# Attention with routed experts: routing units spread over the steps by parity, and the experts' first transposes moved ahead of a value product

## The chip, the cores and the metric

The kernel runs on one core of one Trainium2 chip. The metric is the device time of one execution in microseconds (us), from the median of several runs.

## The reference, cut to what matters

```python
scores = scale * q @ k.T                     # B=4, H=8, S=768, D=64
scores = where(sink | window, scores, -1e9)  # 4 sink keys, the last 128 keys
a = exp(scores - max) / (sum + 1e-9)
x = (a @ v), heads side by side              # 3072 tokens x 512
g = argmax(x @ w_group); e = argmax(x @ w_expert[g])   # 4 groups x 4 experts
out[token] = p(g) * p(e) * (relu(x @ w1[g, e]) @ w2[g, e])
```

Every token goes to one expert of 16, with 512 inputs, 1024 hidden units and 512 outputs.

## The kernel before, in words

**Attention** is a loop of 26 steps (L1234). Steps 0 to 23 each start one tile of 128 queries of all 8 heads (six tiles to a batch element), and each works on three tiles at once: scores, row maxima and exponentials of tile i, transposes and value products of tile a = i-1, and the end of tile b = i-2. Every engine takes its instructions strictly in the order in which the loop writes them.

TensorE's order in a step is: `scores(i,0)`, `values(b,1)`, `scores(i,1)`, `sink_t(a)` and `trans(a,1)` (transposes of the probabilities), `natural(b)` (the output turned back into rows), `logits(b)`, `values(a,0)`, the routing batch's matmuls if there are any, `sink_values(a)`, `trans(i,0)`. In the trace these are `ps<-kb,qb`, `po<-pw,vv`, `tp<-ident,sp`, `tp<-ident,pt`, `po<-ident,xT`, `ps<-wsd,xT`, `tp<-oh,trib` and its followers, and `po<-spT,sv`.

VectorE's order is: `maxima(i,0)`, `maxima(i,1)` (`sm<-ps,msk`, after a copy `ps<-selu,ps`), in even steps `sums` (`rc`), `norm_logits(b)` (`lw<-ps,rc`), then `norm(b)` (`xt<-po,rc`), which divides the rows by their sums and lets the tile go to memory. `norm` reads the same banks of `po` that the next step's `values(b,1)` writes. ScalarE does the exponentials (`pt<-sm,st`), copies transposes out of PSUM (`evac`: `pw<-tp`; `sink_evac`: `spT`; `out_evac`: `xT<-po`) and the rounded halves of the experts' weights (`whi`); VectorE makes the rest of these weights (`wlo`) in steps from 18 on. GpSimd multiplies the probabilities by a triangular mask (`halves`: `pw<-pw,tri`, two a step) and adds up the heads' logits.

**Routing** is done in four batches of six tiles. `route_batch` (L364) is a generator whose pieces, the units, are small VectorE instructions. Their order is: maximum `m`, difference `d`, `req`, second maximum `m2`, comparison `eq`, one-hot `oh`; the matmuls ("pe"); `pe` and a copy of the counts ("rd"); for batches 1 and 2 the choice of an expert, `pick_id` (`ktmp`, `cs`, `key`, `ktop`, `ktmp`, `keid`, `eid`, `oh01`); `rs`, `runb`, `pos`, `ge`, `gs`, `ga`, `m0`, `rm`, `s5`, `rss`; two units HV1 and HV2 ("hv": `bf` on VectorE, `af` on GpSimd); matmuls ("pe") and the addition to the table `tab` ("rd"); `sel` and `index` (`gidx`, `idz`, `sidx`). Batches 0 to 2 become ready in steps 8, 14 and 20. Batches 0 and 1 keep intermediate tensors in free columns of the scores' PSUM tile `psb[1]` (`keep`, L376); batch 2 keeps most of them in SBUF.

A step has places at which units are taken:

```python
maxima(i, 1, lambda k: unit(k) if k else None)   # L1299: two units
routing(1, ("pe",))                              # L1316
for k in range(4): unit(k)                       # L1327: four, ahead of norm
norm(b)                                          # L1330
late()                                           # L1335: wlo of a weight chunk
routing(1, ("rd",)); routing(1, ("hv",))         # L1336, L1337
for k in range(2): unit(k)                       # L1338: two more
```

**The experts' entry.** In steps 24 and 25 the attention is finished while the first expert's work begins: `early_work` (L1215) transposes two gathered tiles of tokens (`ph<-ident,xg`, copied by ScalarE and VectorE into `un`) and then runs the first layer in pieces. After that the experts follow one another, TensorE reading weights as pairs `whi` and `wlo`.

Of the kernel before, what the change touches and what calls it, by code (L numbers as in the profile page):

```python
# [55 lines left out]
XLEAD = 9  # L56
PEGAP = 1.6
REND, TSTEP = 8, 16
UNITS = {}
HC = 3  # L60
LATE = 6
PELAG = 2.0
# [72 lines left out]
def moe_attention(tc, kqT, vN, vS, nsw, wgx, w1, w2, out):  # L135
    nc = Pinned(tc)
    v = nc.vector
    with ExitStack() as top, ExitStack() as att:
# [41 lines left out]
        def bank(pt):  # L180
            return pt.tile([P, 4, P], F32, name="tp")
# [7 lines left out]
        def spare():  # L189
            return tail[0].tile([P, 512], F32, name="ph")  # L190
# [162 lines left out]
        def put_gates(n):  # L353
            for _ in range(min(n, len(gates))):
                t, g = gates.pop(0)
                nc.sync.dma_start(xd[t * P:(t + 1) * P, DM:XW], g)
# [7 lines left out]
        def route_batch(i0, nb, lt, wk, pt, tab, na, pick=None):  # L364
# [35 lines left out]
            yield  # L400
            v.tensor_reduce(m, o5a, AX.X, ALU.max)
            yield
            og = psb[1][:, :, PART - nb:PART].rearrange("p c n -> p n c") if keep else o5[:, :, 0]
            if keep:
                o5b, mb = (t.rearrange("p a (b k) c -> p a b k c", k=nk) for t in (o5a, wide(m)))
                v.tensor_tensor(og.rearrange("p (a b) c -> p a b c", a=na2), o5b[:, :, :, 0], mb[:, :, :, 0], ALU.is_equal)
            v.tensor_tensor(o5a, o5a, wide(m), ALU.is_equal)
# [1 line left out]
            oh = wk.tile([P, nb, NE], BF16, name=f"oh{nb}", bufs=1)  # L409
            v.tensor_tensor(oh.rearrange("p n (g e) -> p n g e", g=G), o5[:, :, 1:],  # L410
                            og[:, :, :, None].to_broadcast([P, nb, G, EG]), ALU.mult)
            yield "pe"
            pp = misc(pt)
            pc = pp[:, nb * NE:(nb + 1) * NE]
# [458 lines left out]
        def values(i, g):  # L873
            pw = env[i]["pw", g]
            new, old = vts[i], vts.get(i - 1) if i % NT else None
            quarters(g, 0, P, new[:, 0], lambda d, j: pw[d, 2 * j:6 + 2 * j:5], start=g == 0)
            quarters(g, D, D, new[:, 1], lambda d, j: pw[d, 1 + 2 * j], stop=g == 1 and old is None)
            if old is not None:
                quarters(g, 0, P, old[:, 1], lambda d, j: pw[d, 4 + 2 * j:10 + 2 * j:5])
                quarters(g, 0, D, old[:, 0], lambda d, j: pw[d, 8 + 2 * j], stop=g == 1)  # L880

        def out_evac(i):
            env[i]["xT"] = xT = wk.tile([P, NDC, P], F32, name="xT", bufs=1)
            nc.scalar.copy(xT.rearrange("p (g l) q -> p l g q", l=2), po2[:, :, 0:256].rearrange("p l (g q) -> p l g q", g=2))
# [85 lines left out]
        def xpose(q, j, early=False):  # L970
            T, o = q["T"], q["o"]
            w = min(P, T - j * P)
            src = xg[q["r"], q["j0"] + j]
            cg[q["r"], q["j0"] + j] = gate = gp.tile([P, 1], F32, name="cg", bufs=10)
            tx = spare().rearrange("p (a b) -> p a b", a=NDC) if early else bank(ps_t)
            dve(0.3 + 0.5 * w / P)
            for c in range(NDC):
                nc.tensor.transpose(tx[:, c, 0:w], src[0:w, c * P:(c + 1) * P], ident[0:w, 0:w])
            if q["plain"]:
                q["x"] = a = yp.tile([P, NDC, 64], F32, name="xr", bufs=1)[:, :, 0:w]  # L980
                nc.scalar.copy(a, tx[:, :, 0:w])
                v.tensor_copy(gate[0:w], src[0:w, DM:DM + 1])
                return
            a = xx[:, :, o + j * P:o + j * P + w]
            nc.scalar.copy(a, tx[:, :, 0:w])
            v.tensor_tensor(xx[:, :, o + T + j * P:o + T + j * P + w], tx[:, :, 0:w], a.bitcast(F32), ALU.subtract)
            v.tensor_copy(gate[0:w], src[0:w, DM:DM + 1])
# [226 lines left out]

        def early_work(q):  # L1215
            plan.update(todo=[], at=0, next=0)
            for j in range(q["nt"]):
                xpose(q, j, True)
                yield 0.43
            for k, us in enumerate(layer1_wide(q)):  # L1220
                if k == LATE:
                    wait_for("late")
                    xpose(PARTS[0][1], 0, True)
                yield us
# [3 lines left out]
        def unit(k):  # L1228
            if quota[0] > 0 and routing(1, (None,)):
                quota[0] -= 1  # L1230

        ew = early_work(PARTS[0][0])
        load_s(0)
        for i in range(NI + 2):  # L1234
            live = i < NI
            quota[0] = UNITS.get(i, REND)
            a, b = i - 1, i - 2
            mid, old = 0 <= a < NI, 0 <= b < NI
            state["clk"] += 3.0
            if i == NI:  # L1240
                flush()
                state.update(gap=0.0, dve=state["clk"])
                sps.close()
                put_gates(MAXB)
                while later:
                    gather(*later.pop(0))
                ps_h = fl.enter_context(tc.tile_pool(name="ps_h", bufs=4, space=PSUM, side="right", reuse_waits="tile"))
                tail.append(ps_h)
            if live:
                scores(i, 0)  # L1250
            if mid:
                evac(a, 0)
            if i == NI and half:
                half.pop()()()
            if old:
                if b < NI - 1:
                    values(b, 1)
                out_evac(b)
            if live:
                load_v(i)  # L1260
                scores(i, 1)
                issue()
                maxima(i, 0)
                warm(FILL[i] if i < len(FILL) else 0, tp2[:, 0, 256:448])
            if mid:
                sink_copy(a)
                halves(a, 0)
            if i == NI + 1:
                state["at"] = 0.0
                routing(1, ("pe",))  # L1270
            if mid:
                if not live:
                    next(ew)
                    next(ew)
                sink_t(a)
                trans(a, 1)
            if live:
                exps(i, 0, (0, 1))
            if mid:
                evac(a, 1)  # L1280
                sink_evac(a)
            if live:
                exps(i, 0, (2, 3))
            if mid and not live:
                halves(a, 1)
            if not live and later and not gates:
                gather(*later.pop(0))
            late = None
            if live:
                late = half.pop()() if half else wjob()  # L1290
                if half and i % NT == 0:
                    first, more = late, half.pop()
                    late = lambda: (first(), more()())
            if i == 0:
                late_consts()
            if i == 1:
                routing_consts()
            if live:
                maxima(i, 1, lambda k: unit(k) if k else None)  # L1299
            if old:  # L1300
                natural(b)
            state["clk"] += 3.0
            if old:
                logits(b)
            if live and mid:
                values(a, 0)
            if i % 2 == 0 and 0 < i <= NI:
                sums(i - 1)
            if not live:
                norm(b)  # L1310
                norm_logits(b)
                next(ew)
            if mid and not live:
                values(a, 0)
            add_heads()
            routing(1, ("pe",))  # L1316
            if mid:
                sink_values(a)
            if live and old:
                norm_logits(b)  # L1320
            if live:
                if mid:
                    halves(a, 1)
                flush()
                exps(i, 1)
                trans(i, 0)
                for k in range(4):  # L1327
                    unit(k)
                if old:
                    norm(b)  # L1330
                if later and not gates:
                    gather(*later.pop(0))
                put_gates(2)
                if late:
                    late()  # L1335
                routing(1, ("rd",))  # L1336
                routing(1, ("hv",))  # L1337
                for k in range(2):  # L1338
                    unit(k)
            else:  # L1340
                if mid:
                    values(a, 1)
                    next(ew)
                put_gates(MAXB)
                routing(TSTEP, (None, "rd", "hv"))
            if old:
                del env[b]
            if i >= CHOOK:
                prefetch(min(RAW, len(raws) + (1 if live else RAW)))
            if not live:  # L1350
                wjob()
                next(ew, None)
# [295 lines left out]
```

## Time and profile before

| | us |
|---|---|
| median of 3 runs | 487.92 |
| lowest and highest run | 487.7, 488.58 |
| the profiled execution | 487.55 |
| its span, first to last instruction | 485.7 |
| TensorE busy | 462.8 (95%) |
| VectorE busy | 341.5 (70%) |
| ScalarE busy | 325.9 (67%) |
| GpSimd busy | 163.8 (34%) |

The span is what the trace covers; 1.85 us of the profiled execution lie around it. Attention takes the first 147 us or so, the experts the rest. An engine's idle time before an instruction is printed in brackets in the timeline, with what ended it.

### The profile page before, as it was taken

To read this page: it belongs to the slowest core of one execution; us is meant where nothing else is said; L and a number is where in the kernel's file an instruction comes from. 1 tells how busy PE (TensorE), PEld (TensorE's weight loads), DVE (VectorE), ACT (ScalarE), POOL (GpSimd) and SP (SyncE) were. 2 spreads that over 40 slices of the span, in tenths; PEclk is the share of its full clock that TensorE was granted. 3 is DMA by queue.
4 is the path that set the end of the run, shared out by engine and by line. 5 is a ranking of instruction groups with operands and counts; after the bars stand their busy time and mean duration, and the time that the engine had idled before them with its cause. 6 is when DMAs were issued, how large, how long until landed. Compare 5 with 4: busy or idle time off the path is not lost.

```text
span 485.7 us, 15514 instructions
## 1 busy us (share of the span) xinstructions
PE 462.8 (95%) x5865; PEld 394.7 (81%) x5865; DVE 341.5 (70%) x1143; ACT 325.9 (67%) x875; POOL 163.8 (34%) x269
## 2 busy tenths in 40 slices
PE   7999999998879999999999999999999999999994
PEld 6887778776768987989888778797979788877894
DVE  6766787888897799893075256563788888788870
ACT  4898889889884353772265275655778787687961
POOL 3463675565656022323203033012402160205021
PEclk9999999999999999999999999999999999999999
DMA  6566567577764469795124388858969997968200
GB/s 192 162 200 206 192 181 215 181 232 259 263 203 137 132 202 360 242 360 217 47 70 148 109 282 289 306 218 305 381 216 373 410 384 249 301 210 298 63 26 31
DMA packets 49556, 107.47 MB, mean 221 GB/s; under 512 B 8932, under 2 KB 9444, under 8 KB 49472
## 3 DMA queue, kind: packets, MB, share of 16 engines
q1 hardware_dynamic: 45008, 93.17, 56.7%
q0 software_dynamic: 4320, 12.94, 7.7%
q8 instruction: 48, 0.79, 0.7%
q10 hardware_dynamic: 144, 0.28, 0.2%
q14 instruction: 36, 0.29, 0.2%
HBM read 93.58 MB, written 12.93 MB: 219 GB/s over the span
## 4 chain that ended last, share of the span: by engine, by line
PE 65%; DVE 13%; issue 8%; ACT 6%; DMA 4%; POOL 2%; SPq 1%; POOLq 0%; DVEq 0%; ACTq 0%
PE po L105 29%; PE ph L105 28%; PE tp L105 4%; PE ps L105 4%; DVE wlo L105 3%; ACT pt L105 2%; DVE sm L105 2%; DVE xt L105 2%; ACT whi L105 1%; DMA rw<-in_w 1%; DVE un L105 1%; DMA vv<-in_vN 1%; DVE ps L105 1%; DMA ni<-in_nsw 1%; SPq L105 1%
## 5 line engine op out<-in xcount | busy, mean ns | idle before, releaser
L105 DVE TENSOR_TENSOR wlo<-rw,whi 128x1024 fp32r<-128x1024 f32 (+1 forms) x116 | 134.9, 1187 | 28.3 <-ACT whi L105 27.9
L105 PE MATMUL ph<-un,whi 128*128 128x256 f32 (+9 forms) x576 | 128.8, 313 | 0.1
L105 PE MATMUL po<-whi,un 128*128 128x512 f32 (+6 forms) x384 | 126.3, 394 | 0.0
L105 ACT CAST whi<-rw 128x1024 fp32r<-128x1024 f32 (+1 forms) x116 | 114.8, 1018 | 5.7 <-PE po L105 3.5
L105 POOL DMA_INDIRECT out<-ot,sidx x33 | 41.7, 1264 | 221.0 <-ACT ot L105 164.3
L105 PE MATMUL ph<-un,wlo 128*128 128x160 f32 (+10 forms) x416 | 99.6, 265 | 0.2 <-DVE wlo L105 0.2
L105 PEld LDWEIGHTS ph<-un,whi 128*128 128x128 f32 x576 | 94.0, 189 | 2.4 <-issue 0.6
L105 PEld LDWEIGHTS po<-whi,un 128*128 128x128 f32 (+5 forms) x384 | 69.8, 183 | 19.3 <-issue 2.1
L105 ACT ACTIVATE pt<-sm,st 128x136 f32<-128x136 f32 x192 | 76.2, 404 | 7.9 <-DVE st L105 7.7
L105 PE MATMUL po<-wlo,un 128*128 128x512 f32 (+7 forms) x200 | 77.9, 389 | 0.0
L105 PEld LDWEIGHTS ph<-un,wlo 128*128 128x128 f32 x416 | 76.8, 190 | 0.8 <-DVE wlo L105 0.4
L105 POOL TENSOR_TENSOR pw<-pw,tri 128x512 f32<-128x512 f32 x40 | 51.6, 1289 | 17.9 <-ACT pw L105 17.0
L105 DVE CUSTOM_DVE_ANT_0 sm<-ps,msk 128x136 f32<-128x136 f32 x192 | 46.3, 296 | 7.2 <-ACT xT L105 1.4
L105 PE MATMUL po<-pw,vv 64*64 64x128 f32 (+1 forms) x1408 | 40.9, 250 | 7.0 <-POOL sp L105 2.3
L105 PEld LDWEIGHTS po<-pw,vv 64*64 64x64 f32 x1408 | 34.9, 133 | 13.4 <-POOL sp L105 8.2
L105 POOL DMA_INDIRECT xg<-xd,gidx x33 | 35.1, 1065 | 29.4 <-DMA rw<-in_w 16.1
L105 PE MATMUL ps<-kb,qb 64*64 64x204 f32 (+1 forms) x768 | 41.9, 331 | 3.1 <-DVE bf L105 2.1
L105 PEld LDWEIGHTS po<-wlo,un 128*128 128x128 f32 (+6 forms) x200 | 35.7, 179 | 7.8
L105 DVE TENSOR_TENSOR hc<-ph,hc 128x160 f32<-128x160 f32 (+6 forms) x64 | 21.5, 337 | 26.2 <-ACT hc L105 26.2
L105 ACT ACTIVATE un<-ph 128x256 fp32r<-128x256 f32 (+1 forms) x40 | 15.3, 383 | 36.4 <-PE ph L105 36.0
L105 ACT ACTIVATION_READ_ACCUMULATOR pt<-sm,st 128x1 f32 x192 | 37.2, 194 | 0.0
L105 ACT ACTIVATE ot<-po,cg 128x512 f32<-128x512 f32 (+7 forms) x25 | 17.0, 679 | 29.3 <-PE po L105 29.2
(226 smaller groups left out, 654.6 us busy)
## 6 DMA issues: line engine op xcount, KB each, us to landing
rw<-in_w SPq DMA_DIRECT2D x128, 512.0 KB, 5.9
kb<-in_kqT SPq DMA_DIRECT2D x23, 272.0 KB, 4.6
qb<-in_kqT SPq DMA_DIRECT2D x24, 256.0 KB, 3.7
vv<-in_vN SPq DMA_DIRECT2D x24, 256.0 KB, 3.7
xd<-xt SPq DMA_DIRECT2D x24, 256.0 KB, 2.7
xg<-xd,gidx POOLq DMA_INDIRECT x33, 5.8
out<-ot,sidx POOLq DMA_INDIRECT x33, 5.9
sv<-in_vS SPq DMA_DIRECT2D x4, 128.0 KB, 3.7
```

The costliest lines, as they stand in the source:

```text
L105: r = f(*a, **k)
```

## The change

It takes out `UNITS` (an empty table, so the quota of 8 units a step stays). It gives the comparison that makes `oh` a PSUM operand in batch 2 as well (`early` in place of `keep`), at one more small instruction. In steps with i % 6 = 3 it takes one unit in the middle of `maxima(i,0)`. Ahead of `norm` it takes up to 4 units in odd steps, 2 in even ones and 1 where i % 6 = 2; an "hv" unit may now be taken there and counts four. After `norm` the "rd" unit comes first, then `late` and two units, or the units first where the next one is "hv". In step 24 the transposes of both token tiles, `sink_copy`, the first `halves` and `trans(a,1)` are written ahead of `values(b,1)`, and `evac(a,1)`, the second `halves` and the copies of the token tiles ahead of `out_evac(b)`; the second half of a weight chunk comes after `sink_evac`.

```diff
@@ route_batch
-            og = psb[1][:, :, PART - nb:PART].rearrange("p c n -> p n c") if keep else o5[:, :, 0]
-            if keep:
+            og = psb[1][:, :, PART - nb:PART].rearrange("p c n -> p n c") if early else o5[:, :, 0]
+            if early:
                 o5b, mb = (t.rearrange("p a (b k) c -> p a b k c", k=nk) for t in (o5a, wide(m)))
                 v.tensor_tensor(og.rearrange("p (a b) c -> p a b c", a=na2), o5b[:, :, :, 0], mb[:, :, :, 0], ALU.is_equal)
...
+            og = og if keep else o5[:, :, 0]
             yield "pe"
@@ early_work
-            for j in range(q["nt"]):
-                xpose(q, j, True)
-                yield 0.43
+            both = []
+            for j in range(q["nt"]):
+                both.append(spare().rearrange("p (a b) -> p a b", a=NDC))
+                for c in range(NDC):
+                    nc.tensor.transpose(both[j][:, c], xg[q["r"], j][:, c * P:(c + 1) * P], ident)
+            yield 0.86
+            for j in range(q["nt"]):
+                xpose(q, j, both[j])
+            yield 0.0
@@ a new function
+        def fill(n, kinds=(None, "hv")):
+            while n > 0 and quota[0] > 0:
+                big = bool(rb) and rb[0][2] == "hv"
+                if not routing(1, kinds):
+                    return
+                n -= 4 if big else 1
+                quota[0] -= 1
@@ the loop of steps
-            if i == NI and half:
-                half.pop()()()
+            if i == NI:
+                next(ew)
+                sink_copy(a)
+                halves(a, 0)
+                trans(a, 1)
             if old:
                 if b < NI - 1:
                     values(b, 1)
+                if i == NI:
+                    evac(a, 1)
+                    halves(a, 1)
+                    next(ew)
                 out_evac(b)
+            if i == NI:
+                sink_t(a)
+                sink_evac(a)
+                if half:
+                    half.pop()()()
...
-                maxima(i, 0)
+                maxima(i, 0, lambda k: unit(k) if k == 1 and i % NT == 3 else None)
...
-                for k in range(4):
-                    unit(k)
+                fill((2, 1, 4)[i % 2 * 2 if i % NT != 2 else 1])
                 if old:
                     norm(b)
...
+                routing(1, ("rd",))
+                if late and not (rb and rb[0][2] == "hv"):
+                    late()
+                    late = None
+                    kinds = None,
+                else:
+                    kinds = None, "hv"
+                fill(2, kinds)
                 if late:
                     late()
-                routing(1, ("rd",))
-                routing(1, ("hv",))
-                for k in range(2):
-                    unit(k)
```

The calls of step 24 that stand earlier now (`sink_copy`, `halves`, `sink_t`, `trans`, `evac`, `sink_evac`) are taken out of their old places, which the other steps keep.

## Rows read from the trace of the kernel before

**Rows 1.** Windows: length, busy PE, PEld, DVE, ACT, POOL; clock, DMA, GB/s.

```profile
49.40:55.90 6.50, 5.45 (x150) 4.52 (x146) 5.71 (x30) 4.89 (x22) 5.08 (x8) 1.00 0.51 182
...
150.00:250.00 100.00, 99.09 (x708) 88.59 (x707) 67.96 (x191) 45.94 (x81) 26.93 (x32) 1.00 0.59 200
```

**Rows 2.** Timeline of PE, steps 8 and 9: start, length, instruction, idle before.

```profile
54.94 0.90 PE L105 MATMUL po<-pw,vv 64*64 64x128 f32 x32 [1.05 <-DVE ps L105]
...
57.77 0.90 PE L105 MATMUL po<-pw,vv 64*64 64x128 f32 x32
58.60 0.22 PE L105 MATMUL tp<-oh,trib 128*128 128x96 bf16 x1
```

**Rows 3.** Timeline of DVE, steps 8 and 9.

```profile
52.97 0.28 DVE L105 TENSOR_REDUCE ps<-lt 128x30 f32<-128x120 f32 x1
...
54.11 0.68 DVE L105 TENSOR_TENSOR xt<-po,rc 128x512 f32<-128x512 f32 x1
...
55.23 0.26 DVE L105 TENSOR_TENSOR oh<-req,ps 128x96 bf16<-128x96 f32 x1
...
59.75 0.69 DVE L105 TENSOR_TENSOR xt<-po,rc 128x512 f32<-128x512 f32 x1 [1.13 <-ACT pt L105]
```

**Rows 4.** Timelines of PE and DVE, steps 10 and 16.

```profile
66.93 0.90 PE L105 MATMUL po<-pw,vv 64*64 64x128 f32 x32 [0.53 <-DVE row L105]
...
100.26 0.33 DVE L105 TENSOR_REDUCE ps<-oh 128x16 f32<-128x96 bf16 x1
...
101.57 0.90 PE L105 MATMUL po<-pw,vv 64*64 64x128 f32 x32 [0.80 <-DVE xt L105]
```

**Rows 5.** Waits of PE, 44 to 150 us (total, times, longest); one DVE row.

```profile
PE ps L105 <- DVE bf L105: 2.1, 2, 1.6
...
PE ps L105 <- DVE sidx L105: 0.8, 1, 0.8
...
111.19 0.69 DVE L105 TENSOR_TENSOR xt<-po,rc 128x512 f32<-128x512 f32 x1 [0.89 <-PE po L105]
```

**Rows 6.** Timelines of DVE, POOL and ACT, steps 21 to 24.

```profile
132.77 1.33 DVE L105 TENSOR_TENSOR oh<-req 128x96 bf16<-128x96 f32 x1
...
140.10 0.17 DVE L105 SCALAR_TENSOR_TENSOR key<-cnt,col 128x16 f32<-128x16 f32 x1
...
143.25 0.82 DVE L105 SCALAR_TENSOR_TENSOR ktmp<-key,ktop,col 128x16 f32<-128x16 f32 x1
...
144.97 0.17 DVE L105 TENSOR_TENSOR runb<-runb,rs 128x16 bf16<-128x16 bf16 x1
...
138.23 0.69 DVE L105 TENSOR_TENSOR xt<-po,rc 128x512 f32<-128x512 f32 x1 [0.49 <-DMA rw<-in_w]
...
146.60 1.01 DVE L105 TENSOR_TENSOR ge<-row,edge 128x48 f32<-128x48 f32 x1
...
132.58 1.41 POOL L105 TENSOR_TENSOR pw<-pw,tri 128x512 f32<-128x512 f32 x1 [0.28 <-ACT pw L105]
...
140.54 1.29 POOL L105 TENSOR_TENSOR pw<-pw,tri 128x512 f32<-128x512 f32 x1 [0.96 <-ACT pw L105]
...
139.88 0.58 ACT L105 COPY pw<-tp 128x512 f32<-128x512 f32 x1 [0.47 <-DVE cnt L105]
```

**Rows 7.** Timelines of PE and ACT, step 24.

```profile
145.92 0.90 PE L105 MATMUL po<-pw,vv 64*64 64x128 f32 x32 [1.67 <-POOL sp L105]
146.75 1.09 PE L105 MATMUL ph<-ident,xg 128*128 128x128 f32 x8
...
148.13 0.41 PE L105 MATMUL po<-ident,xT 64*128 64x64 f32 x8
...
145.49 0.57 ACT L105 COPY pw<-tp 128x512 f32<-128x512 f32 x1
...
146.87 0.59 ACT L105 COPY xT<-po 128x512 f32<-128x512 f32 x1 [0.30 <-PE po L105]
147.44 1.07 ACT L105 CAST un<-ph 128x512 fp32r<-128x512 f32 x2
```

More of the change, by code (lines that the diff above doesn't have):

```diff
@@ L58 @@
 REND, TSTEP = 8, 16
-UNITS = {}
 HC = 3
@@ L974, in xpose @@
             cg[q["r"], q["j0"] + j] = gate = gp.tile([P, 1], F32, name="cg", bufs=10)
-            tx = spare().rearrange("p (a b) -> p a b", a=NDC) if early else bank(ps_t)
+            tx = early if early not in (True, False) else spare().rearrange("p (a b) -> p a b", a=NDC) if early else bank(ps_t)
             dve(0.3 + 0.5 * w / P)
-            for c in range(NDC):
+            for c in range(NDC if early in (True, False) else 0):
                 nc.tensor.transpose(tx[:, c, 0:w], src[0:w, c * P:(c + 1) * P], ident[0:w, 0:w])
@@ L1235, in moe_attention @@
             live = i < NI
-            quota[0] = UNITS.get(i, REND)
+            quota[0] = REND
             a, b = i - 1, i - 2
@@ L1262, in moe_attention @@
                 issue()
-                maxima(i, 0)
+                maxima(i, 0, lambda k: unit(k) if k == 1 and i % NT == 3 else None)
                 warm(FILL[i] if i < len(FILL) else 0, tp2[:, 0, 256:448])
-            if mid:
+            if live and mid:
                 sink_copy(a)
@@ L1270, in moe_attention @@
                 routing(1, ("pe",))
[L1271 to L1274, printed above, removed]
+            if live and mid:
                 sink_t(a)
@@ L1278, in moe_attention @@
                 exps(i, 0, (0, 1))
-            if mid:
+            if live and mid:
                 evac(a, 1)
@@ L1283, in moe_attention @@
                 exps(i, 0, (2, 3))
-            if mid and not live:
-                halves(a, 1)
             if not live and later and not gates:
```

## The prediction

> **What bounds the kernel now.** I read the windows first, one step of attention and then the stretch behind it. In the step from 49.4 to 55.9 us no engine is full: TensorE is busy for 5.45 of 6.5 us [rows 1]. From 150 to 250 us TensorE is busy for 99.09 of 100 us [rows 1]. So whatever attention and the experts' entry gain or lose moves the end one for one. Next I read TensorE's timeline for its idle time. In step 9 (the even steps' sums have just been made) `values` starts after 1.05 us of idle time [rows 2]. The timeline of VectorE names the cause: `norm` (`xt<-po,rc`) starts at 54.11, behind four units, and ends at 54.79; `values`, which writes the banks that `norm` reads, follows 0.15 later [rows 2, 3]. Step 14 repeats this pattern; steps 10 and 16 lose 0.53 and 0.80 us in the same place [rows 4]. In the steps with weight work two other waits stand out: scores wait 2.1 us in all for `bf` and 0.8 for `sidx` [rows 5], since those read `psb[1]`. Last, I looked for VectorE instructions that are longer than their like. `oh` takes 1.33 us in batch 2 where it takes 0.26 in batch 0, `ktmp` 0.82 and `ge` 1.01; each lies beside a GpSimd multiply of some 1.3 us and ends with it [rows 3, 6]. Only batch 2, whose operands both lie in SBUF, shows this.
>
> **The parts, step by step** (later is +).
>
> *Steps 8 and 14: 0.* One unit instead of four stands ahead of `norm`. `m` ends at 53.25, so `norm` can start 0.94 us earlier than 54.11 and `values` too [rows 2, 3]. But `m2`, `eq` and `oh` now lie among the maxima of the next step, and the routing matmuls follow in that same step, ahead of `sink_values`. VectorE has the same six units and two maxima to do before those matmuls as before, in another order, with `oh` at the end; before, that work was done when `lw` started, which was ahead of an idle 1.13 us up to the `norm` at 59.75 [rows 3]. `m2` must also wait for scores that share its bank. By this count `oh` ends at about 58.45 and the matmul starts 0.15 later, at 58.6; it started at 58.60 before, right behind `values` at 57.77 [rows 2]. TensorE's wait has moved from `norm` to the one-hot. Bounds: -0.94 and +0.2 each.
>
> *Step 10: -0.25.* Two units leave the front of `norm`; of the 0.53 us [rows 4] some 0.45 can go. HV1 and HV2 now fall into one step, so GpSimd does two `af` ahead of the next `sink_copy` and `halves`, which gives back 0.2. Bounds -0.53 and 0.
>
> *Step 16: -0.47.* `rs` (0.33) and `runb` (0.17, priced by batch 2's) go behind `norm` [rows 4, 6], less a little overlap. Bounds -0.80 and 0.
>
> *Steps 18 to 20: -0.25.* HV1 moves into the 0.89 us that VectorE idles before `norm` in step 18 [rows 5] and HV2 ahead of the weights' `wlo`, so the 2.1 us of waiting for `bf` go. VectorE's queue, not the scores, then sets the next step, and the table matmuls, `tab`, `sel` and `index` come one step earlier: the 0.8 us for `sidx` [rows 5] come back there. Bounds: -2.1 and +0.6.
>
> *Steps 20 and 21: +0.64.* As in step 8 the one-hot gates the routing matmuls, now in step 21 rather than 22, so that what the last three parts won is nearly used up at the `norm` of step 21. Bounds 0 and +0.9.
>
> *Step 21 behind `norm`: +0.68.* Before, `wlo` and the held `oh` took 1.9 us until the next maxima, 1.33 of it `oh`. With the one-hot's operand in PSUM the 1.07 us of excess go. In its place come `pe`, `cnt`, `wlo`, `ktmp`, `cs` and two `key`. ScalarE's `evac` waits for `cnt`, takes 0.58, and the multiply starts 0.08 behind it (140.54 against 139.88 + 0.58, [rows 6]); with 0.1 from `cnt` to `evac` that is 0.76 after `cnt`. `wlo` and the two small ones, now behind `cnt`, take some 0.83, and then comes `key`, which reads two SBUF tensors: it waits for the multiply's 1.29 [rows 6]. From `norm` on this makes 0.35 for `pe` and `cnt`, 0.76, 1.29 and 0.2 for the second `key`: 2.6 against 1.9. The 0.83 and the 0.35 are my estimates from the small instructions' 0.17 to 0.25 and what is left of the 1.9. Bounds: -1.07 (no meeting) and +0.8.
>
> *Step 22: +0.5, then +0.5.* In this step with sums nothing stood ahead of `norm`; now `ktop`, `ktmp` (0.82 beside a multiply, [rows 6]), `keid`, `eid` and `oh01` do, some 1.2 us with overlap; 0.49 of that was idle [rows 6] and 0.2 more is taken off as the routing matmuls have left the step. Behind `norm`, `wlo`, `rs` and `runb` replace `wlo` and six short instructions. `evac` no longer waits for `cnt` (0.47, [rows 6]), so the multiply is under way when `runb` (0.17 when free) wants to read two SBUF tensors. Bounds of each: 0 and +1.3.
>
> *Step 23: -0.15.* `ge` beside a multiply replaces `ktmp` beside one, the rest is equal in size.
>
> *Step 24: +0.8.* TensorE idled 1.67 us before `values` [rows 7]; the tokens' transposes (1.09) and `trans` now lie in that time. But `xT`, on which `natural` waits, now stands behind more on ScalarE: from the end of the exponentials at 145.5, `evac` 0.57, `trans` 0.42 with two waits of 0.1 (it shares the banks that `evac` reads), `evac` 0.57, the casts 1.07, `xT` 0.59 and 0.1 to TensorE [rows 7]: 148.9, where `natural` was at 148.13. VectorE and ScalarE shift a little against each other, hence -0.05. Behind it TensorE's work is the same. The weight casts that go later are covered by this wait. Bounds: -1.0 (all of the transposes' 1.09 saved) and +1.2. The batch's earlier progress costs nothing and buys nothing: its matmuls in step 25 waited for nothing.
>
> The sum is -0.25 - 0.47 - 0.25 + 0.64 + 0.68 + 0.5 + 0.5 - 0.15 + 0.8 = **+2.0 us**, on the profiled execution's 487.55: 489.55. The median of the runs stands 0.37 above that execution, so I forecast 489.9.
>
> *A rule beside the rows.* Three instructions were held by 1.07, 0.6 and 0.8 us, a mean of 0.82; priced so, `key` and `runb` together would cost 0.7 us less than I put. The Trainium skill, SBUF — State Buffer, "Who interferes with whom", says that an instruction of VectorE with two SBUF inputs and a reading one of GpSimd lock each other out for the whole instruction, whichever began first. By that rule both wait out what is left of the multiply, as in the sum above; by the mean alone the time would be 489.2. The ends of `oh` and of its multiply (134.10 and 133.99, [rows 6]) agree with the rule.
>
> **The rivals.**
>
> *No meeting.* If VectorE gets to `key` and `runb` before the multiplies begin (`key` misses by 0.07 us in my count), the 0.68 and one 0.5 fall away: 489.9 - 1.2 = 488.7, within 0.2% of before. For it: `key` ran freely at 140.10 [rows 6]. Against: `runb` misses by 0.4.
>
> *Faster.* VectorE is ahead of my count by some 0.7 us in each batch, because TensorE's earlier scores let it start sooner. Its place is the one-hot in steps 9, 15 and 21. From 0.7 us on, the routing matmuls find it ready, and the 0.94, 0.94 and 0.64 us stay won; batch 2 then slips ahead of its multiplies too, another 1.2: 489.9 - 3.7 = 486.2. For it: VectorE idles 1.13 us in step 9 [rows 3], so it isn't full. Against: that idle time lies behind the one-hot, not ahead of it.
>
> *Step 24 as meant.* If `trans` needn't wait for `evac` and `xT` gets through, the entry gives -1.0 instead of +0.8: 488.1, no change.
>
> **How the numbers follow.** The three runs span 0.9 us, so about 0.2% (1 us) can be told from no change. The forecast has 0.48, the two rivals near zero 0.20 together, the faster one 0.32. The slower side reaches to 491.4 if both held instructions take the upper bounds; the faster one to 485.2, with the entry's gain on top. Outside that I leave 2 in 10. Alone, the likeliest case runs from 489.0 to 491.4.
>
> **What would show it.** Right: in steps 9 and 15 `values` without the 1.05 us of idle time, and an idle stretch of some 0.5 us before `tp<-oh,trib` instead; `oh` of batch 2 at 0.26; a `key`, `runb` or `ge` of over 0.8; in step 24 the tokens' transposes before `values` and TensorE waiting over 1 us for `xT`. Wrong: routing matmuls that start without waiting in step 9, steps 21 to 23 no longer than before, or `natural` in step 24 less than 3 us behind the exponentials.

## The result, and the profile after

The changed kernel takes **492.99 us** in the median of four runs (491.41 to 494.5), beside 487.81 for the kernel before in the same comparison: a ratio of **1.0105 [1.0069, 1.0141]**. It is slower, as forecast, but by 5.2 us and not by 2, and outside the range.

The profiled execution is the shortest of the four, 491.41 us. Its page begins with the span and the busy times, then the span in 40 slices of 12.24 us:

```profile
span 489.6 us, 15516 instructions
...
PE 466.1 (95%) x5865; PEld 397.0 (81%) x5865; DVE 341.5 (70%) x1144; ACT 325.6 (66%) x875; POOL 164.7 (34%) x269
...
PE   7999999997888999999999999999999999999994
...
PEclk9999999999988999999999999999999999999998
```

Against the table of before, VectorE, ScalarE and GpSimd are as busy as they were. TensorE has the same 5865 instructions but 3.3 us more busy time, and the line of its clock shows why: two slices, from 135 to 159 us, are not at full clock (the third is the very end). The page of before has a 9 in every slice.

To see where the 3.9 us of span came from, I took the starts of `xT<-po` from ScalarE's timeline, one for each step, and compared their distances:

| from `xT` of step to step | before, us | after, us | difference | forecast |
|---|---|---|---|---|
| start to 8 (nothing changed) | 49.44 | 48.66 | -0.78 | 0 |
| 8 to 10 | 12.15 | 12.12 | -0.03 | 0 |
| 10 to 12 | 11.60 | 11.26 | -0.34 | -0.25 |
| 12 to 14 | 10.53 | 10.73 | +0.20 | none |
| 14 to 16 | 12.41 | 12.84 | +0.43 | 0 |
| 16 to 18 | 11.78 | 11.43 | -0.35 | -0.47 |
| 18 to 22 | 25.41 | 25.84 | +0.43 | +0.39 |
| 22 to 23 | 7.05 | 8.59 | +1.54 | +1.68 |
| 23 to 24 | 6.51 | 8.51 | +2.00 | +0.65 |
| 24 to 25 | 9.91 | 10.50 | +0.59 | 0 |

Up to step 22 each line holds to half a microsecond, and from step 8 on they add up to +0.34 where the forecast has -0.33. (Ahead of step 8 the profiled executions of all these kernels differ by up to 0.8 us, so the first line is scatter.) Most of what is missing lies in the last two lines, +2.59 against +0.65. They are best taken together: the forecast of step 24 was counted at `natural`, which in the kernel before began 0.67 us behind the end of `xT`.

**Steps 8 and 9.** TensorE's timeline of after, to be read beside [rows 2]:

```profile
53.21 0.90 PE L104 MATMUL po<-pw,vv 64*64 64x128 f32 x32
...
57.79 0.22 PE L104 MATMUL tp<-oh,trib 128*128 128x96 bf16 x1 [0.66 <-ACT pt L104]
```

And VectorE's:

```profile
52.38 0.68 DVE L104 TENSOR_TENSOR xt<-po,rc 128x512 f32<-128x512 f32 x1
...
57.48 0.25 DVE L104 TENSOR_TENSOR oh<-req,ps 128x96 bf16<-128x96 f32 x1
```

`norm` starts right behind the first unit, and `values` no longer waits. But `oh` ends at 57.73, and the routing matmul starts 0.06 later, after 0.66 us of idle time (the bracket names ScalarE, whose `pt` was done before; the one-hot came last). The wait has moved from `norm` to the one-hot, and the two steps together are as long as before (12.12 against 12.15 us).

**Steps 21 to 23.** VectorE's timeline, of batch 2's instructions only:

```profile
129.40 0.25 DVE L104 TENSOR_TENSOR oh<-req,ps 128x96 bf16<-128x96 f32 x1
...
132.76 1.28 DVE L104 SCALAR_TENSOR_TENSOR key<-cnt,col 128x16 f32<-128x16 f32 x1
...
137.14 0.69 DVE L104 SCALAR_TENSOR_TENSOR ktmp<-key,ktop,col 128x16 f32<-128x16 f32 x1
...
140.56 0.91 DVE L104 TENSOR_TENSOR runb<-runb,rs 128x16 bf16<-128x16 bf16 x1
```

And the multiplies of GpSimd in the same stretch:

```profile
132.74 1.28 POOL L104 TENSOR_TENSOR pw<-pw,tri 128x512 f32<-128x512 f32 x1 [1.56 <-ACT pw L104]
...
136.51 1.29 POOL L104 TENSOR_TENSOR pw<-pw,tri 128x512 f32<-128x512 f32 x1 [1.53 <-ACT pw L104]
...
140.02 1.42 POOL L104 TENSOR_TENSOR pw<-pw,tri 128x512 f32<-128x512 f32 x1 [0.28 <-ACT pw L104]
```

`oh` is down from 1.33 [rows 6] to 0.25. In its place `key` begins 0.02 us behind a multiply and ends with it, `ktmp` ends with the second, and `runb` with the third. Behind `key` wait the scores' copy and maxima of step 22, and behind these, by 1.60 us, TensorE's `logits`.

**Step 24.** ScalarE's timeline of after, to be read beside [rows 7]:

```profile
146.49 0.57 ACT L104 COPY pw<-tp 128x512 f32<-128x512 f32 x1
148.53 0.58 ACT L104 COPY pw<-tp 128x512 f32<-128x512 f32 x1 [1.47 <-PE po L104]
149.01 1.08 ACT L104 CAST un<-ph 128x512 fp32r<-128x512 f32 x2
149.97 0.62 ACT L104 COPY xT<-po 128x512 f32<-128x512 f32 x1
```

And TensorE's:

```profile
145.28 1.09 PE L104 MATMUL ph<-ident,xg 128*128 128x128 f32 x8
147.11 0.47 PE L104 MATMUL tp<-ident,pt 64*128 64x64 f32 x8 [0.75 <-ACT pw L104]
147.51 0.90 PE L104 MATMUL po<-pw,vv 64*64 64x128 f32 x32
...
150.64 0.46 PE L104 MATMUL po<-ident,xT 64*128 64x64 f32 x8 [1.10 <-ACT xT L104]
```

The tokens' transposes stand ahead of `values`, as they should, and TensorE then waits for `xT`. `natural` begins 4.05 us behind the last exponential (2.54 before; the sum of the prediction gave 3.4). The line that I had not counted on is the second copy: it waited 1.47 us, not for `trans`, which ended at 147.58, but until `values(22,1)` was done at 148.41. The tiles `pw` have two buffers, and the second half of tile 23 gets the one that `values(22,1)` is still reading.

**The clock.** Windows of after, cut where the granted clock changes (length; busy PE, PEld, DVE, ACT, POOL; clock, DMA share, GB/s):

```profile
133.00:135.75 2.75, 1.15 (x30) 0.72 (x23) 2.68 (x12) 1.13 (x4) 1.82 (x4) 1.00 0.83 231
135.75:137.33 1.58, 1.58 (x50) 1.46 (x52) 1.44 (x11) 1.58 (x9) 0.82 (x1) 1.00 0.74 271
137.33:140.74 3.41, 3.21 (x40) 2.65 (x44) 3.17 (x11) 2.61 (x11) 2.41 (x4) 0.50 0.29 67
...
147.00:150.98 3.98, 1.91 (x50) 1.59 (x50) 1.84 (x7) 2.51 (x7) 3.29 (x6) 1.00 0.79 208
150.98:154.40 3.42, 3.42 (x31) 3.29 (x28) 2.03 (x7) 0.28 (x1) 3.19 (x7) 0.50 0.44 95
```

In two stretches TensorE was granted 0.50 of its clock, 1.2 of 2.4 GHz. Ahead of each lies a stretch with waits, in which it was busy for 1.15 of 2.75 us and for 1.91 of 3.98 us; the first fall came only after another 1.58 us in which TensorE was full. In the slow stretches TensorE is all but full and needs longer for the same: scores 1.64 where they take 0.92, a pair of first-layer matmuls (`ph<-un,whi`) 0.63 where before takes 0.40. Before had nothing of this kind until the last 2.2 us of its span, when TensorE has no work left.

So there are three suspects: VectorE's held instructions, ScalarE's order in step 24, and the halved clock, which the other two may set off.

### The profile page after: what moved, and what is told of

It is laid out like the page before. It is cut to its first block, busy times and chain, and to the rows that moved or that the text cites. A ratio compares the mean times of both kernels' runs of the same rounds, so it can differ in the third digit from the quotient of the medians.

```text
span 489.6 us, 15516 instructions
## 1 busy us (share of the span) xinstructions
PE 466.1 (95%) x5865; PEld 397.0 (81%) x5865; DVE 341.5 (70%) x1144; ACT 325.6 (66%) x875; POOL 164.7 (34%) x269
## 3 DMA queue, kind: packets, MB, share of 16 engines
q0 software_dynamic: 4320, 12.94, 7.6%
## 4 chain that ended last, share of the span: by engine, by line
PE 57%; DVE 9%; issue 7%; ACT 5%; POOL 1%; DMA 1%; POOLq 0%; SPq 0%; DVEq 0%; ACTq 0%
PE ph L104 28%; PE po L104 24%; PE tp L104 3%; DVE wlo L104 3%; ACT pt L104 2%; ACT whi L104 2%; PE ps L104 1%; POOL out L104 1%; DVE un L104 1%; DMA qb<-in_kqT 1%; DVE sm L104 1%; ACT un L104 1%; DVE xt L104 1%; DVE big L104 1%; ACT pw L104 1%
```

## The experiments

Each ratio is to the kernel before, run in turn on the same chip (medians 486.94, 487.32 and 487.04 us in the three sittings).

### 1. Step 24 alone, and the units alone

`e_tail` is the kernel before with the new order of step 24 and no other edit; `e_units` is the changed kernel with the old order of step 24.

```diff
@@ e_tail, on the kernel before
-            if i == NI and half:
-                half.pop()()()
+            if i == NI:
+                next(ew)
+                sink_copy(a)
+                halves(a, 0)
+                trans(a, 1)
...
+                if i == NI:
+                    evac(a, 1)
+                    halves(a, 1)
+                    next(ew)
...
@@ e_units, on the changed kernel
-                next(ew)
-                sink_copy(a)
-                halves(a, 0)
-                trans(a, 1)
...
-                if i == NI:
-                    evac(a, 1)
-                    halves(a, 1)
-                    next(ew)
...
```

> The kernel before with the new order of step 24 alone. Theory (the loss is made of held VectorE instructions and added units in steps 21 to 23, of xT standing behind the token copies on ScalarE in step 24, and of the halved TensorE clock that follows the idle time): 488.6 us, +0.8 against 487.8; natural in step 24 some 0.8 us further behind the exponentials, clock not halved before step 24. Rival (the whole loss is the entry's): 492 to 493. Rival (the entry fills the wait for norm): 486.8.

> The change without the new order of step 24. Theory: 490 to 492, steps 22 and 23 about 8 us long each, key, ktmp, runb and ge held as in the changed kernel, and a halved clock near step 22. Rival (the loss is the entry's): 487 to 488, no halved clock.

`e_tail` took 489.91 us, a ratio of 1.0058 [1.0041, 1.0075]; `e_units` 488.92, 1.0036 [1.0020, 1.0052]. The two add up to 0.94%, which agrees with the change's 1.05% within the intervals, so nothing here shows that its parts act on each other. `e_units` costs less than the theory put on it and `e_tail` more: the larger part is step 24, with 2.8 us where I had 0.8. ScalarE's second copy waits 1.47 us in `e_tail` too, and `natural` begins 4.04 us behind the exponentials. Both profiles have a stretch at half clock, `e_units` in step 19, where after has none:

```profile
113.00:115.53 2.53, 1.44 (x38) 1.26 (x41) 2.46 (x14) 1.62 (x7) 1.34 (x4) 1.00 0.70 223
115.53:122.35 6.82, 6.82 (x83) 5.92 (x86) 3.99 (x21) 4.26 (x18) 1.83 (x4) 0.50 0.51 161
```

The same windows of `e_tail`, in step 24:

```profile
146.50:149.84 3.34, 1.39 (x35) 1.08 (x27) 2.06 (x6) 2.73 (x6) 2.54 (x6) 1.00 0.56 165
149.84:153.25 3.41, 3.41 (x26) 3.19 (x28) 1.66 (x6) 0.38 (x1) 0.70 (x2) 0.50 0.57 170
```

From step 19 to 21 `e_units` needs 14.74 us, where after needs 12.94 without such a stretch: 1.8 us lost. This is no accident of one execution. Of the eight profiles here of kernels with the spread units, four (`e_units`, `e_key_first`, `e_xt_first`, `e_pw`) have the same 6.8 us at half clock in step 19 and take 14.74 or 14.75 us; the six without the spread units never do and take 12.83 or 12.84. In all eight TensorE waits twice in step 19, 0.94 to 0.96 us for GpSimd's `sp` and 0.5 us ahead of `logits`; in the six it waits once, some 1.6 us for `bf`. In step 22, where after has its first stretch, `e_units` runs at full clock: 7.89 us from `xT` to `xT` against 8.59.

### 2. VectorE's held instructions

`e_og` takes one edit of the change alone, batch 2's one-hot operand in PSUM. `e_psum` is the changed kernel with batch 2's counts, `key`, `rs` and `pos` in PSUM too. `e_key_first` leaves them in SBUF and puts the units of step 21 ahead of `wlo`.

```diff
@@ e_og, on the kernel before
-            og = psb[1][:, :, PART - nb:PART].rearrange("p c n -> p n c") if keep else o5[:, :, 0]
-            if keep:
+            og = psb[1][:, :, PART - nb:PART].rearrange("p c n -> p n c") if early else o5[:, :, 0]
+            if early:
...
+            og = og if keep else o5[:, :, 0]
@@ e_psum, on the changed kernel
-            pos, ga = (psb[1][:, x, PART + ny:PART + ny + nb] if keep else
+            pos, ga = (psb[1][:, x, PART + ny:PART + ny + nb] if (early, keep)[x] else
...
-                n_e = psb[1][:, 3, PART:PART + NE] if keep else cnt
+                n_e = psb[1][:, 3, PART:PART + NE] if early else cnt
...
-                yield from pick_id(wk, pick, n_e, keep)
-            rs = psb[1][:, 1, PART:PART + NE] if keep else
+                yield from pick_id(wk, pick, n_e, early)
+            rs = psb[1][:, 1, PART:PART + NE] if early else
...
@@ e_key_first, on the changed kernel
-                if late and not (rb and rb[0][2] == "hv"):
+                if late and i != 21 and not (rb and rb[0][2] == "hv"):
```

> The kernel before with the one-hot's PSUM operand in batch 2 alone. Theory: oh falls from 1.33 to 0.26, step 22's maxima start 1.07 us earlier, the time falls by 0.7 to 1.1 to about 486.9. Rival (another wait takes its place, the logits or the next norm): 487.8, no change.

> The changed kernel, with batch 2's key, counts, rs and pos in PSUM, so that key, ktmp, runb and ge read one SBUF tensor at most. Theory (the held instructions of batch 2 are part of the loss): key, ktmp, runb and ge each take 0.17 to 0.40 us beside GpSimd's multiplies instead of 1.29, 0.69, 0.91 and 0.40; steps 21 to 23 come out 1.3 to 2.5 us shorter in all, and the time is 490.5 to 491.7 against the changed kernel's 493.0. Rival (these instructions are covered by other waits): they are short, steps 21 to 23 keep their length, 492.5 to 493.5.

> The changed kernel, with the units of step 21 written ahead of the weights' wlo, so that key gets to VectorE before GpSimd's multiply begins. Theory: key takes 0.17 to 0.25 us instead of 1.29, wlo (several SBUF operands) goes beside the multiply; step 21 to 22 is up to 1.1 us shorter, 491.9 to 492.5. Rival: wlo is held in key's place, or key still meets the multiply, and nothing moves: 492.8 to 493.5.

`e_og` took 486.56 us, 0.9996 [0.9977, 1.0014]: no difference that can be told, though in its profile the step from 22 to 23 is 0.92 us shorter and that from 21 to 22 is 0.22 longer.

`e_psum` took 490.18 us, **1.0060 [1.0046, 1.0073]**, 2.2 us less than the changed kernel's 1.0105 would give, though the two intervals overlap a little; the trace says it more surely. VectorE's timeline (`key` is now `ps<-ps,col`):

```profile
132.74 0.17 DVE L104 SCALAR_TENSOR_TENSOR ps<-ps,col 128x16 f32<-128x16 f32 x1
...
138.86 0.17 DVE L104 TENSOR_TENSOR runb<-runb,ps 128x16 bf16<-128x16 bf16 x1
```

GpSimd's multiplies in it:

```profile
132.73 1.27 POOL L104 TENSOR_TENSOR pw<-pw,tri 128x512 f32<-128x512 f32 x1 [1.57 <-ACT pw L104]
...
138.82 1.28 POOL L104 TENSOR_TENSOR pw<-pw,tri 128x512 f32<-128x512 f32 x1 [0.18 <-ACT pw L104]
```

The same instructions at the same moment, 0.01 and 0.04 us behind the same multiplies, with one operand in PSUM: 0.17 us each, where they took 1.28 and 0.91. The step from 22 to 23 falls from 8.59 to 6.23 us. Of these 2.36 us some 0.7 are the stretch at half clock (8.59 against the 7.89 of `e_units`), which is gone with the 1.60 us wait, and 1.66 the held instructions themselves. (The clock falls in this profile too, for 6.8 us behind 147.5, and from `xT` 24 to `xT` 25 it needs 11.62 us.)

`e_key_first` took 492.28 us, 1.0095 [1.0076, 1.0114], no clear gain. `key` does run in 0.17 us, and the step from 22 to 23 comes to 6.80. But its profile has stretches of 6.8 us at half clock in steps 19 and 24. The times run from 490.78 to 493.42, the profiled execution being the longest. VectorE's and GpSimd's timelines show the other half of the mechanism:

```profile
134.87 0.68 DVE L104 TENSOR_TENSOR wlo<-rw,whi 128x512 fp32r<-128x512 f32 x1
...
135.03 1.67 POOL L104 TENSOR_TENSOR pw<-pw,tri 128x512 f32<-128x512 f32 x1 [0.82 <-ACT pw L104]
```

Here `wlo`, with two operands in SBUF, had begun first, from 134.87 to 135.55, and the multiply took 1.67 us instead of 1.28. The Trainium skill, SBUF — State Buffer, "Who interferes with whom", says that whichever of the two engines begins first keeps the shared ports for the whole instruction, and the other is blocked; these rows agree, in both orders.

### 3. ScalarE's order in step 24

`e_xt_first` is the changed kernel with `out_evac`, which makes `xT`, ahead of the casts of the tokens. `e_pw` gives the second half of tile 23 a buffer of its own.

```diff
@@ e_xt_first
-                    next(ew)
                 out_evac(b)
+                if i == NI:
+                    next(ew)
@@ e_pw
-            e["pw", g] = pw = wk.tile([P, 12, D], F32, name="pw", bufs=2)
+            z = (i, g) == (NI - 1, 1)
+            e["pw", g] = pw = wk.tile([P, 12, D], F32, name="pwz" if z else "pw", bufs=1 if z else 2)
```

> The changed kernel with out_evac written ahead of the two token tiles' copies in step 24. Theory: natural starts about 1 us earlier behind the exponentials, TensorE's wait of 1.10 us for xT falls below 0.2; 0.8 to 1 us less than the changed kernel, about 492. Rival (the first layer then waits for the token copies instead): no gain, 493.

> The changed kernel, with a buffer of its own for the second half of tile 23's probabilities, so that its copy out of PSUM need not wait until values(22,1) has read the old one. Theory (that buffer is the part of step 24 that the prediction missed): the wait of 1.47 us of ScalarE ahead of this copy falls to some 0.5, xT and natural come 0.7 to 0.9 us earlier, from 4.1 to some 3.3 us behind the exponentials, 492.0 to 492.4. Rival (ScalarE waits for the transposes or the casts for the tokens just as long): natural within 0.2 us of 4.1 behind the exponentials, 492.8 to 493.2.

`e_xt_first` took 491.93 us, 1.0092 [1.0059, 1.0126], which can't be told from the change's own. `natural` comes 1.0 us earlier (3.06 behind the exponentials), but the first layer then waits 0.50 us for the tokens' copies on VectorE, and the clock falls there.

`e_pw` took 491.0 us, 1.0066 [1.0046, 1.0085], about 1.9 us less than the change, though the intervals overlap and the executions, from 488.92 to 493.07, move with the clock; the trace says it more surely. ScalarE's timeline:

```profile
150.78 0.59 ACT L104 COPY pwz<-tp 128x512 f32<-128x512 f32 x1 [0.56 <-PE tp L104]
```

The wait falls from 1.47 to 0.56 us and is now one for `trans`, as the prediction had it; `natural` comes 3.14 us behind the exponentials, near the 3.4 that I had worked out. So this buffer is the part of step 24 that I missed. From `xT` 23 to `xT` 25 this profile needs 16.82 us, with no slow stretch in it (it has two earlier ones, in steps 19 and 22), against after's 19.01 and before's 16.42.

### 4. The clock

`e_warm` fills the places where TensorE waits with matmuls that compute nothing (zeros by zeros):

```diff
-                warm(FILL[i] if i < len(FILL) else 0, tp2[:, 0, 256:448])
+                warm(FILL[i] if i < len(FILL) else 12 if i in (21, 22, 23) else 0, tp2[:, 0, 256:448])
...
+                warm(12, tp2[:, 0, 0:192])
                 sink_t(a)
```

> The changed kernel, with 12 small matmuls without use (zeros by zeros into a free part of the transposes' banks) in steps 21, 22 and 23 behind the first maxima, and 12 in step 24 ahead of the sink's transposes. Theory (TensorE's idle stretches of 1 us and more in these steps bring its granted clock to half, at 1.1 to 1.2 us of loss for each stretch of 3.4 us): the windows from 130 us to the end of step 25 show a clock of 1.00, scores and the first layer keep their full-speed lengths, and the time is 490.5 to 492 against 493.0, with less spread between runs. Rival (the clock costs nothing on the path, or the filler costs as much as it saves, 12 matmuls being some 1 us a step): 492.8 to 495.

It took 490.96 us, 1.0080 [1.0064, 1.0095]: 1.2 us less than the change by the ratios, whose intervals overlap, although each twelve cost TensorE 1.15 us. By the profiles it needs 26.46 us from `xT` 22 to `xT` 25, fillers included, and after 27.60. Five of its six executions have a mean clock of 0.997 to 0.999, where the changed kernel's four have 0.986 to 0.993. The windows of its profile:

```profile
130.00:148.00 18.00, 15.91 (x374) 13.39 (x368) 15.73 (x67) 14.11 (x55) 10.65 (x17) 1.00 0.65 208
148.00:160.00 12.00, 11.09 (x192) 10.12 (x190) 5.56 (x15) 4.97 (x11) 6.75 (x12) 1.00 0.46 138
```

The clock stays at 1.00, while `key` (1.27) and `natural` (4.04 behind the exponentials) are as late as ever. With TensorE's idle time filled and nothing else mended the clock stays up: the halved clock is a loss of its own, and in these steps it hangs on TensorE's idle time.

### 5. All of it mended, and the best of both

`e_mended` joins `e_psum`, `e_pw` and `e_xt_first`. `e_keys` is the kernel before with batch 2's operands in PSUM (all but `pos`, which is still read when `psb[1]` has been given up). `e_entry` is the kernel before with the tokens' transposes alone ahead of `values`; `e_best` is `e_keys` and `e_entry` together.

The transposes themselves are split off in `early_work` as in the change; the loop of `e_entry` and `e_best` reads:

```diff
@@ e_entry and e_best, the loop of steps
+            if i == NI:
+                next(ew)
             if old:
                 if b < NI - 1:
                     values(b, 1)
...
                 if not live:
                     next(ew)
-                    next(ew)
```

> The changed kernel with all three mended: batch 2's operands in PSUM, a buffer of its own for the second half of tile 23's probabilities, and xT ahead of the casts for the tokens. Theory (held instructions and the order of ScalarE's work in step 24, with the stretches at half clock that follow them, are the whole loss of 1.05%): 0.1 to 0.4% above before, natural 2.6 to 3.0 us behind the exponentials, no stretch at half clock between 130 and 160 us. Rival (the spreading of the units costs something of its own, or the clock falls all the same): 0.5 to 0.8% above before.

> The kernel before, with batch 2's one-hot operand, counts, key and rs in PSUM, and nothing else of the change. Theory (an instruction of VectorE is held by GpSimd's multiply where both its tensors are in SBUF): oh 0.25 instead of 1.33, ktmp 0.2 instead of 0.82, ge stays at 1.0 since its operands stay in SBUF; steps 22 to 24 together 0.9 to 1.6 us shorter, 0.2 to 0.3% less time than before. Rival (what VectorE gains is idle time there): short instructions, the same time within 0.15%.

> The kernel before, with the tokens' transposes alone ahead of values(22,1) in step 24; trans, the copies out of PSUM and the casts for the tokens stay where they were. Theory (of the new order of step 24 the loss comes from putting trans and the copies of tile 23 ahead of the end of tile 22, not from the tokens' transposes): the transposes lie in the 1.67 us that TensorE waits ahead of values, natural comes 2.0 to 2.4 us behind the exponentials instead of 2.54, and the time is 0 to 0.12% less than before. Rival (the tokens' transposes or casts are the loss): natural over 2.6 us behind the exponentials and a time above that of before by 0.1% or more.

> The two edits above together: batch 2's operands in PSUM and the tokens' transposes ahead of values, in the order of the kernel before. Theory: the gains add up, 0.2 to 0.4% less time than before. Rival: either gain is idle time on TensorE, or the clock falls in some runs and takes it back, within 0.15% of before.

`e_mended` took 487.2 us, **1.0017 [1.0001, 1.0034]**: of the change's 1.05% all but 0.17 are gone. Seven of its twelve executions have a mean clock of 0.996 to 0.998 and a median of 486.93 us, beside before's 487.04; the other five (0.990 to 0.993) take 488.06 to 489.62. So in an execution whose clock stays up the spreading of the units costs nothing, and wins nothing. But five of twelve with a lower clock are many: of the 35 executions of the kernel before in the same sitting only one lies below 0.994. No trace of the five was kept; step 19, where four profiles with spread units have their slow stretch, is the likely place, but that is not shown. (`natural` comes 2.52 us behind the exponentials, as early as before.)

`e_keys` took 486.16 us, **0.9977 [0.9964, 0.9990]**: 0.23% faster than the kernel before, and the only version whose interval lies below 1. In its profile the three steps from 21 to 24 are 1.04 us shorter. (`ge`, which I had expected to be held, fell between two multiplies and took 0.21. The weights' `wlo` behind it, which also reads two SBUF tensors, met the second one and took 1.37 us.)

`e_entry` took 487.24 us, 0.9996 [0.9985, 1.0007]. The tokens' transposes do no harm: `natural` comes 1.91 us behind the exponentials, 0.63 earlier than before. But the distance from `xT` 24 to `xT` 25 stays at 9.91 us, since the first layer's second group of matmuls then waits 0.66 us for `un`, which VectorE makes behind `wlo`. `e_best` (487.41 us, 0.9996 [0.9982, 1.0009]) should have added up the gains and did not. TensorE's timeline of it in step 24:

```profile
147.29 0.38 PE L105 MATMUL ph<-un,whi 128*128 128x256 f32 x1
148.49 0.58 PE L105 MATMUL ph<-un,whi 128*128 128x256 f32 x1 [0.82 <-DVE un L105]
```

And its windows:

```profile
146.30:148.46 2.16, 1.37 (x25) 1.06 (x25) 2.16 (x6) 1.56 (x4) 1.01 (x2) 1.00 0.94 256
148.46:151.87 3.41, 3.38 (x31) 3.16 (x35) 1.51 (x6) 0.38 (x1) 1.87 (x6) 0.50 0.63 222
```

`natural` now comes 1.53 us behind the exponentials, a whole microsecond earlier than before. VectorE's `un` doesn't, TensorE waits 0.82 us for it, and then the clock falls. VectorE's timeline says why `un` is late:

```profile
145.80 1.38 DVE L105 TENSOR_TENSOR wlo<-rw,whi 128x512 fp32r<-128x512 f32 x1 [0.32 <-ACT whi L105]
...
147.76 0.67 DVE L105 TENSOR_TENSOR un<-ph,un 128x512 fp32r<-128x512 f32 x1
```

This `wlo` lies beside a multiply that GpSimd began at 145.32, and takes 1.38 us where it takes 0.68 in `e_entry`: with batch 2's instructions out of the way, a larger one of the queue is held in their place. (No run moves this `wlo`.) Four executions without such a fall (mean clock 0.997 and 0.998) take 486.17 to 486.34 us, eight with it (0.991 to 0.994) 487.10 to 488.31, with a median of 487.7. The difference, 1.4 us, prices one such stretch behind step 24, if the seven without a trace lose their clock where the profiled one does. Even the four are no faster than `e_keys`.

## Why the prediction was wrong

The direction and most of the mechanisms held; the sum was short, mainly by one term that was too small and one that was missing. In its order:

- **Steps 8 and 14: 0.** The wait moved from `norm` to the one-hot, as written. Steps 8 and 9 gave -0.03; steps 14 and 15 gave +0.43, above the bound of +0.2, and no run shows what made it.
- **Steps 10 and 16: -0.25 and -0.47.** -0.34 and -0.35. In step 10 nothing is left of the wait ahead of `values`; in step 16 it is 0.35 where it was 0.80.
- **Steps 18 to 21: -0.25 and +0.64.** Together +0.43 up to `xT` 22 against +0.39. The 2.1 us of waiting for `bf` did go, and `sidx` costs 1.0 us. Steps 12 and 13, of which the prediction says nothing, gave +0.20.
- **Steps 21 and 22 behind and ahead of `norm`: +1.68.** `key` met the multiply, `ktmp` and `runb` too: 1.28, 0.69 and 0.91 us long. Without them these steps would have been shorter than before (6.23 against 7.05 in `e_psum`), so the term at full clock is +0.84 (7.89, `e_units`, against 7.05). The measured +1.54 agrees with the forecast by accident: 0.7 of it is the clock. The rule of the whole instruction was the right one against the mean of 0.82. That only batch 2's instructions can be held was too narrow: `wlo` can, as `e_best` shows.
- **Step 23: -0.15.** `ge` took 0.40 in place of 1.01. In after no separate size can be read off, since the next `xT` lies in step 24; in `e_units`, which has the old step 24 and a full clock there, the step from 23 to 24 took 6.90 us against 6.51, so +0.39.
- **Step 24: +0.8.** This is the step that failed. The chain on ScalarE was put down as copy, `trans`, copy, casts, `xT`, with `trans` alone between the copies. The second copy waits for `values(22,1)` as well, whose buffer it takes over: `natural` comes 4.05 us behind the exponentials instead of 3.4, and 3.14 once the copy has a buffer of its own (`e_pw`). Against before's 2.54 that is +1.5 for +0.8.
- **The missing term: the clock.** "Behind it TensorE's work is the same" was true of the instructions and not of their durations. By the rows above, the stretch in step 22 cost 0.7 us and the one behind step 24 some 1.4 (24 to 25: 10.50 against 9.07 in `e_pw` and 9.13 in `e_warm`, where none fell). Together 2.1 of the 4.5 us by which the profile of after falls behind from step 8 to step 25, where the forecast had 2.0. The median of the four executions stands another 1.6 us above the profile. Two of the others have a mean clock of 0.986 against the profile's 0.989, and a stretch in step 19, as in the profile of `e_units`, costs 1.8; but the fourth took 492.55 us at 0.993, so the clock can't be all of this gap. No trace of those executions exists, and the rest of the gap stays open.
- **The range.** The upper end of 491.4 is not the sum named for it: `key` at +0.8 and `runb` at +1.3 give 489.9 + 0.12 + 0.8 = 490.8, and only both parts of step 22 at +1.3 come near it (491.5). The measured 492.99 lies above all of these.

Of the rivals, the faster one needed the one-hot early, and it was not: the matmul waited 0.66 us. "No meeting" fell with `key`, which missed the multiply's start by 0.02 us (my count had 0.07). "Step 24 as meant" would not have given its -1.0 in any case: `e_entry` and `e_best` bring `natural` forward by 0.6 and 1.0 us, and the next wait, VectorE's `un`, takes it back.

## What to carry to other kernels

When an instruction is moved ahead of others, ask not only what it waits for but whose buffer it takes over: a copy into a tile with two buffers waits for the reader of the one before last, wherever that stands in the order. A small VectorE instruction with both operands in SBUF should not lie beside GpSimd's reads; putting one operand into PSUM brought 0.23% without any other edit. That moves the meeting on, though: look which instruction of the queue lies beside the next read. And a wait of TensorE in a dense stretch has to be priced above its length: it can halve the clock of what follows.

## What the runs showed of the hardware that I had not expected

That stretches with waits of 0.5 to 1.6 us, in a kernel whose TensorE is 95% busy, can be followed by a granted clock of 0.50 for 3.4 or 6.8 us, at a price of 0.7 us (step 22 of after) to 2.5 us (step 24 of `e_psum`, 11.62 against 9.07 in `e_pw`) each. The Trainium skill, TensorE: Matmul & The Clock Gate, Part 1, says that a gate passes half or all of the clock according to how busy the array has been; the two levels agree with the rows here. What the runs don't settle is when. A wait of 1.60 us ahead of `logits` in step 22 was followed by the slow stretch in after; the same wait of 1.59 us in `e_units` was not. In the kernel before, TensorE stands still for most of the stretch from 113 to 115 us, and the clock stays up:

```profile
113.00:115.00 2.00, 0.46 (x12) 0.43 (x16) 1.64 (x4) 1.25 (x3) 1.84 (x5) 1.00 0.69 154
```

Executions of one kernel differ in this: by their mean clock, `e_best` has four without and eight with it. That may be part of why the changed kernel's runs scatter over 3.1 us where the kernel before in the same comparison has 1.35, but its execution with the highest mean clock was not its shortest.
